# Seven block products on two halves of a 512-token group instead of on pairs of groups, w_out resident in SBUF, and the weight conversion's products on VectorE

## The chip, the cores and the metric

The kernel runs on one core of a Trainium2 chip. The metric is the device time of one execution in microseconds (us); lower is better. The engines are named as in the profile: PE (TensorE matmul), PEld (its weight loads), DVE (VectorE), ACT (ScalarE), POOL (GpSimd), SP (SyncE, which only issues DMAs here).

## The reference

Three layers follow each other: linear attention with an RMS norm, a top-1 mixture of experts, and a wide layer with a cosine gate. The change is in the third, and in the preparation of its weights.

```python
kv = einsum('bhsd,bhse->bhde', k, v); out = einsum('bhsd,bhde->bhse', q, kv)
x = rms_norm(out) * g_norm                    # 4608 tokens x 512
expert_idx = argmax(x @ w_gate, axis=1)       # 8 experts, one for each token
ye = relu(xe @ w1[e]) @ w2[e]; x = gate_w * ye
h = x @ w_in                                  # 512 -> 2048
y = (h * cos(h)) @ w_out                      # 2048 -> 512
```

`w_in` and `w_out` arrive as 64-bit floats (8 MB each), all else in float32.

## The kernel before

Each float32 operand of a large product is split into a high and a low part that TensorE multiplies at full rate; high x high, high x low and low x high (`PASS`) are accumulated. So every product of one 128x128 weight tile is three matmuls.

**Expert stage (205 to 648 us of the trace).** The experts run in an order of falling load, each with a first product (`emit_f1`, L289, eight chunks of two halves) and a second one (`emit_f2`, L302). ACT takes relu of a result (L291) and DVE its low part (L292). Between them the program lays other work by hand: DVE splits w2 (L220), ACT and POOL split the next expert's w1 (L207, L208), POOL gathers the next tokens (L256), and `prep()` advances a generator that converts `w_in` and `w_out` from their 64-bit form, one small chunk at a call. In a chunk DVE takes exponent and mantissa apart (L850 to L866), ACT makes floats of them (L871, L873), POOL multiplies (L874, L875: 64 products of 128x512) and, for `w_in`, forms sums of blocks on POOL (L897: 16 of 128x512; L905 to L908: 32 of 128x256). The results go to DRAM (`win`, `wout`).

**Last stage (648 us to the end).** `x @ w_in` is computed by Strassen's method in Winograd's form: two blocks of K (256 each), two blocks of the 2048 columns, and two blocks of tokens give seven products instead of eight. In the first 512-token group (`p == 0`) the token blocks are its two halves, so a matmul has 256 columns. The other eight groups are taken in four pairs (`quads`): the token blocks are whole groups, and a matmul has 512 columns. A step `(p, q)` is 84 matmuls of 256 columns or 42 of 512, read from a ring `wi` of five tiles that POOL's DMA queue fills (L998, L1002). The seven results are added into four blocks C11, C12, C21, C22 (DVE, L1294 to L1333; one goes through ACT L1317 and POOL L1318). For each block DVE and ACT compute the cosine (`emit_cos`: DVE L1197, L1198, L1200, ACT Abs and Sin L1202, L1203), DVE multiplies it in (L1206), ACT and DVE split the result (L1221, L1226), and PE multiplies it by `w_out` (`emit_g2`, L1245, twelve matmuls of 512 columns for a block, accumulated in four PSUM banks of a group). A pair has 32 such blocks, sixteen of its first group and then sixteen of its second; blocks of the second group wait in 20 slots. `w_out` is read again for each group through a ring of four tiles (L1011, 144 loads of 512 KB).

The token operands of a pair are loaded (`y_load`), summed on POOL (L972, L979) and split by ACT and POOL (L983, L984) during the pair before: sums in two of its middle steps, one split in its last step but one, and the other six in its last step. One set of operands is shared in a ring of eight places, so that a place is free only when the products of the pair before have read it.

Of the kernel before, what the change touches and what calls it, by code (L numbers as in the profile page):

```python
# [32 lines left out]
def fused_kernel(  # L33
# [13 lines left out]
    nc = tc.nc  # L47
# [787 lines left out]
    def prep_unit(i):  # L835
# [38 lines left out]
        nc.gpsimd.tensor_tensor(out=d[:, 0], in0=mf, in1=ef, op=ALU.mult)  # L874
        nc.gpsimd.tensor_tensor(out=d[:, 1], in0=ml, in1=ef, op=ALU.mult)  # L875
# [13 lines left out]
    def prep_units():  # L889
        G = nc.gpsimd  # L890
        for c in range(C2 // 2):
# [4 lines left out]
            for d, w in ((da, wa), (db, wb)):  # L896
                G.tensor_tensor(out=w.rearrange("p a n -> p (a n)"), in0=d[:, 0].bitcast(F32),  # L897
                                in1=d[:, 1].bitcast(F32), op=ALU.add)
# [6 lines left out]
            G.tensor_tensor(out=wb[:, 1], in0=wb[:, 0], in1=wb[:, 1], op=ALU.add)  # L905
            G.tensor_tensor(out=wb[:, 0], in0=wa[:, 0], in1=wb[:, 0], op=ALU.subtract)
            G.tensor_tensor(out=wa[:, 0], in0=wb[:, 1], in1=wa[:, 0], op=ALU.subtract)
            G.tensor_tensor(out=wa[:, 1], in0=wa[:, 1], in1=wa[:, 0], op=ALU.subtract)  # L908
# [9 lines left out]
    def prep():  # L918
# [471 lines left out]
```

## Time and profile before

| | us |
|---|---|
| median of three runs (lowest, highest) | 1508.56 (1504.46, 1511.31) |
| the profiled execution, its own time | 1508.87 |
| span of its trace, first to last instruction | 1506.5 |
| PE, DVE, POOL, ACT busy in the span | 1356.9, 1145.8, 755.5, 664.9 |
| mean granted TensorE clock | 0.965 of full speed |

The trace has the attention up to about 200 us, the expert stage to 648 us and the last stage to 1498 us, after which only output DMAs run. A busy time counts from an instruction's start to its end, waiting for a port included, so an engine's share is no measure of the work that it has.

### The profile page before, as it was taken

The numbers are of one execution on the slowest core, as the hardware profiler recorded it, in microseconds if no ns is written. First come the engines' busy times: TensorE is split into PE (matmuls) and PEld (weight loads), VectorE is DVE, ScalarE is ACT, GpSimd is POOL, SyncE is SP. The second block draws the span as 40 slices with busy tenths as digits, with TensorE's granted clock in tenths as the row PEclk, the third lists the DMA queues.
The fourth block names the chain that finished last, engine by engine and source line by source line (L and its number), as shares of the span: only waits on it lengthen the run. The fifth ranks groups of instructions, "written<-read, shape, count | busy, mean of one in ns | idle before, by whom it ended". The sixth has DMA issues, their size and how long they took to land.

```text
span 1506.5 us, 22532 instructions
## 1 busy us (share of the span) xinstructions
PE 1356.9 (90%) x7959; PEld 1188.3 (79%) x7959; DVE 1145.8 (76%) x1848; ACT 664.9 (44%) x1308; POOL 755.5 (50%) x869
## 2 busy tenths in 40 slices
PE   7986898999989889967899877999889997999997
PEld 6885788988989889967688656887678876888876
DVE  2898677888787876329979997879887798878751
ACT  4985234454434444414434354433444434434431
POOL 1346347878866656345733446325732347423232
PEclk9998999999999999989999998999989998999999
DMA  9984435676666666575767555767576664666654
GB/s 320 344 278 152 139 121 175 211 229 193 214 215 215 218 207 207 156 227 168 254 207 223 149 146 174 224 184 219 143 242 195 189 206 143 206 186 209 175 179 142
DMA packets 186058, 300.78 MB, mean 200 GB/s; under 512 B 18773, under 2 KB 125317, under 8 KB 184913
## 3 DMA queue, kind: packets, MB, share of 16 engines
q0 software_dynamic: 59392, 191.64, 42.1%
q1 hardware_dynamic: 116624, 97.58, 20.9%
q10 hardware_dynamic: 9920, 10.03, 1.9%
q8 instruction: 66, 1.08, 0.3%
q14 instruction: 56, 0.45, 0.1%
HBM read 247.22 MB, written 51.98 MB: 199 GB/s over the span
## 4 chain that ended last, share of the span: by engine, by line
PE 34%; DVE 12%; POOL 3%; issue 3%; ACT 2%; DMA 1%; POOLq 0%; another core or an unknown queue 0%; DVEq 0%; ACTq 0%
PE acc L1245 19%; PE pr L1186 15%; DVE ni L1197 3%; DVE g L1200 3%; DVE g L1198 2%; POOL xreg L984 2%; DVE g L1206 1%; DMA wi<-win 1%; DVE ha L1322 1%; DVE gg L1226 1%; POOL y L979 0%; ACT wA L983 0%; ACT g L1203 0%; ACT g L1202 0%; POOL wo L1011 0%
## 5 line engine op out<-in xcount | busy, mean ns | idle before, releaser
L1245 PE MATMUL acc<-wo,gg 128*128 128x512 f32 x1728 | 431.2, 400 | 30.8 <-DVE gg L1226 29.2
L1245 PEld LDWEIGHTS acc<-wo,gg 128*128 128x128 f32 x1728 | 331.8, 193 | 110.4 <-DVE gg L1226 35.6
L1202 ACT ACTIVATE g<-g 128x512 f32<-128x512 f32 x144 | 91.0, 632 | 386.9 <-DVE g L1200 386.6
L289 PE MATMUL hp<-xreg,wA 128*128 128x352 f32 (+7 forms) x1536 | 228.1, 308 | 26.5 <-DVE wB L292 25.0
L289 PEld LDWEIGHTS hp<-xreg,wA 128*128 128x128 f32 x1536 | 219.7, 192 | 32.5 <-DVE wB L292 30.7
L302 PE MATMUL yp<-wB,wA 128*128 128x352 f32 (+7 forms) x1536 | 227.5, 306 | 1.8 <-DVE xreg L273 1.5
L302 PEld LDWEIGHTS yp<-wB,wA 128*128 128x128 f32 x1536 | 217.1, 189 | 3.3 <-DVE xreg L273 2.5
L1186 PE MATMUL pr<-wA,wi 128*128 128x512 f32 (+1 forms) x912 | 194.7, 363 | 25.6 <-DMA wi<-win 9.3
L1186 PE MATMUL pr<-xreg,wi 128*128 128x512 f32 x768 | 197.3, 403 | 14.5 <-DVE ha L1333 7.3
L1186 PEld LDWEIGHTS pr<-wA,wi 128*128 128x128 f32 x912 | 154.5, 196 | 54.9 <-ACT p L1317 9.2
L1011 POOL DMA_DIRECT2D wo<-wout x144 | 79.9, 555 | 231.6 <-PE acc L1245 218.8
L1186 PEld LDWEIGHTS pr<-xreg,wi 128*128 128x128 f32 x768 | 147.0, 192 | 51.9 <-DVE ha L1333 9.2
L1226 DVE TENSOR_TENSOR gg<-g,gg 128x512 fp32r<-128x512 f32 x144 | 126.1, 876 | 39.1 <-ACT gg L1221 38.8
L1002 POOL DMA_DIRECT2D wi<-win x128 | 69.4, 543 | 129.0 <-PE pr L1186 124.5
L1200 DVE SCALAR_TENSOR_TENSOR g<-ni,g 128x512 f32<-128x512 int32 x144 | 120.0, 833 | 4.9
L1221 ACT ACTIVATE gg<-g 128x512 fp32r<-128x512 f32 x144 | 87.3, 620 | 44.7 <-PE acc L1245 44.4
L208 POOL TENSOR_TENSOR wA<-w1s,wA 128x512 fp32r<-128x512 f32 x64 | 86.8, 1366 | 39.2 <-ACT wA L207 38.7
L1203 ACT ACTIVATE g<-g,half_pi 128x512 f32<-128x512 f32 x144 | 104.3, 725 | 4.7
L292 DVE SCALAR_TENSOR_TENSOR wB<-hp,wB 128x352 fp32r<-128x352 f32 (+7 forms) x128 | 57.4, 469 | 63.8 <-ACT wB L291 63.7
L291 ACT ACTIVATE wB<-hp 128x352 fp32r<-128x352 f32 (+7 forms) x128 | 52.0, 421 | 82.7 <-PE hp L289 80.3
L1197 DVE TENSOR_SCALAR ni<-hb 128x512 int32<-128x512 f32 x72 | 53.7, 745 | 20.2 <-POOL hb L1318 20.2
L1318 POOL TENSOR_TENSOR hb<-hb,p 128x512 f32<-128x512 f32 x36 | 49.0, 1361 | 32.0 <-ACT p L1317 30.0
(213 smaller groups left out, 2028.1 us busy)
## 6 DMA issues: line engine op xcount, KB each, us to landing
wo<-wout POOLq DMA_DIRECT2D x144, 512.0 KB
wi<-win POOLq DMA_DIRECT2D x124, 512.0 KB
w1s<-in_moe_w_dram SPq DMA_DIRECT2D x64, 256.0 KB
w2s<-in_moe_w_dram SPq DMA_DIRECT2D x64, 256.0 KB
xs<-xo SPq DMA_DIRECT2D x16, 512.0 KB
raww<-in_moe_w_in_dram SPq DMA_DIRECT2D x16, 512.0 KB
win<-xreg POOLq DMA_DIRECT2D x16, 512.0 KB
raww<-in_moe_w_out_dram SPq DMA_DIRECT2D x16, 512.0 KB
```

What stands on the lines that cost most here:

```text
L208: nc.gpsimd.tensor_tensor(out=d[:, 1], in0=t, in1=d[:, 0], op=ALU.subtract)
L289: nc.tensor.matmul(ps, lhsT=wv[:, a, kk, :], rhs=xT[:, b, kk, sl], start=(i == 0 and kk == 0), stop=(i == 2 and kk == KD - 1))
L302: nc.tensor.matmul(ps, lhsT=wv[:, a, kk % 4, :], rhs=hT[:, kk, b, sl], start=(n == 0), stop=(n == 3 * C1 - 1))
L1011: nc.gpsimd.dma_start(wo[n % WO], wout[wo_seq[n]])
L1186: nc.tensor.matmul(ps, lhsT=w[:, a, kk, :], rhs=y[:, b, kk, :], start=(n == 0), stop=(n == 5))
L1197: nc.vector.tensor_scalar(out=ni, in0=h, scalar1=INV_2PI, scalar2=None, op0=ALU.mult)
L1200: nc.vector.scalar_tensor_tensor(out=r, in0=ni, scalar=-PI2_LO, in1=r, op0=ALU.mult, op1=ALU.add)
L1202: nc.scalar.activation(r, r, AF.Abs)
L1203: nc.scalar.activation(r, r, AF.Sin, scale=-1.0, bias=half_pi)
L1221: nc.scalar.activation(gg[:, 0], t, AF.Copy)
L1226: nc.vector.tensor_tensor(out=gg[:, 1], in0=t, in1=gg[:, 0], op=ALU.subtract)
L1245: nc.tensor.matmul(acc[g][t], lhsT=gg[:, a, col * P:(col + 1) * P], rhs=wv[:, b, :], start=(n == 1), stop=(n == 3 * C2))
```

## The change

1. The pairs are gone: all nine groups are computed as the first one was, on two halves, in four steps of 84 matmuls of 256 columns (`steps`, `emit_prod`, L988 in the changed kernel). The blocks C22, C21, C11, C12 of a step belong to the same group and are multiplied by `w_out` in that order. A step's adds are all on DVE (`products`, L1017 to L1039); the detour of one product through ACT and POOL is gone.
2. The operands of the next group are prepared in the three last steps of a group, two, two and three of them at a step (`y_next`, L948 sums and L964 splits, 128x256 each), and have a ring of fourteen places, so that two groups' operands stand side by side. Those of the first group are summed and split on DVE instead of POOL.
3. The first step of the first group is computed inside the last expert's second product.
4. `w_out` stays in SBUF: sixteen loads (four ahead of the loop, four in each of the next three steps) instead of 144.
5. The products and sums of the weight conversion (L874, L875, L897, L905 to L908) go from POOL to DVE.

```diff
-        nc.gpsimd.tensor_tensor(out=d[:, 0], in0=mf, in1=ef, op=ALU.mult)
-        nc.gpsimd.tensor_tensor(out=d[:, 1], in0=ml, in1=ef, op=ALU.mult)
+        nc.vector.tensor_tensor(out=d[:, 0], in0=mf, in1=ef, op=ALU.mult)
+        nc.vector.tensor_tensor(out=d[:, 1], in0=ml, in1=ef, op=ALU.mult)
...
-            G.tensor_tensor(out=wb[:, 1], in0=wb[:, 0], in1=wb[:, 1], op=ALU.add)
+            V.tensor_tensor(out=wb[:, 1], in0=wb[:, 0], in1=wb[:, 1], op=ALU.add)
...
+    NQ = C2 // 4
+    steps = [(g, q) for g in range(NG) for q in range(NQ)]
+    def y_op(g, i):
+        n = 7 * (g % 2) + i
+        t = (xflat, aflat)[n // 8]
+        return t[:, 1024 * (n % 8):1024 * (n % 8) + 1024].rearrange(
+            "p (t k n) -> p t k n", t=2, k=2)
...
+            nc.gpsimd.dma_start(wi[:, n % WI].rearrange("p a t k f -> p a (t k f)"),
+                                win[2 * q:2 * q + 2, :, i].rearrange("c p t k f -> p c (t k f)"))
...
+            add(out=hb[:, 1], in0=hb[:, 1], in1=half["p2"], op=ALU.add)
+            add(out=ha[:, 1], in0=ha[:, 1], in1=half["p4"], op=ALU.add)
...
+                for i in ((), (0, 1), (2, 3), (4, 5), (6,), (), (), ())[u]:
+                    y_split(0, i, nc.vector)
+                for i in ((), (), (), (), (), (0, 1), (2, 3, 4), (5, 6, 7))[u]:
+                    products(0, 0, i)
...
-    gslots = [reg4.tile([P, 512], F32, name=f"g{i}") for i in range(20)]
-    wo = [reg4.tile([P, 2, 512], F32R, name=f"wo{i}") for i in range(WO)]
+    gslots = [reg4.tile([P, 512], F32, name=f"g{i}") for i in range(6)]
+    gg_ring = [wA1[:, 6], wA1[:, 7], reg4.tile([P, 2, 512], F32R, name="gg")]
+    wo = [reg4.tile([P, 2, 512], F32R, name=f"wo{i}") for i in range(C2)]
...
+        products(g, q, 0)
+        if q > 0:
+            y_next(2 * q - 2)
+        emit_g(prev + ("C21",))
+        emit_cos(prev + ("C12",))
+        emit_g(prev + ("C11",))
         emit_split()
         second()
+        products(g, q, 1)
+        if q == 3:
+            y_next(5)
...
+        products(g, q, 4)
+        if q > 0:
+            y_next(2 * q - 1 if q < 3 else 6)
...
+        if q == 0 and g + 1 < NG:
+            y_load(g + 1, wk2)
+        for _ in range(4):
+            if g == 0 and wo_seq:
+                load_wo()
```

Three places show how the instructions moved. On PE at the end of the expert stage (`yp` is the last expert's second product, `pr` a Strassen product, a step's seven being 84 matmuls):

```order
 L302 MATMUL yp<-wB_2156,wA_2161 128x272 x12
 L302 MATMUL yp<-wB_2156,wA_2162 128x272 x12
+L988 MATMUL pr<-xreg,wi 128x256 x48
 L302 MATMUL yp<-wB_2156,wA_2163 128x272 x12
 L302 MATMUL yp<-wB_2156,wA_2164 128x272 x12
+L988 MATMUL pr<-xreg,wi 128x256 x24
 L302 MATMUL yp<-wB_2156,wA_2163 128x272 x12
 L302 MATMUL yp<-wB_2156,wA_2164 128x272 x12
```

Six of the first step's products stand between blocks of the second product, and the seventh follows the last of them; before, all came behind it. On POOL in the last step of a pair, before (L984 is a split, L979 a sum, L1318 the add of one product, `wi` and `wo` loads of weights):

```order
L1002 DMA wi<-win 128x1024
L984 TENSOR_TENSOR wA_170<-yst,wA_170 128x512 x2
L1002 DMA wi<-win 128x1024
L984 TENSOR_TENSOR xreg<-y_9404,xreg 128x512
L984 TENSOR_TENSOR xreg<-y_9405,xreg 128x512
L1011 DMA wo_9399<-wout 128x1024
L984 TENSOR_TENSOR xreg<-t_10464,xreg 128x512
L984 TENSOR_TENSOR xreg<-t_10465,xreg 128x512
L1002 DMA wi<-win 128x1024
L984 TENSOR_TENSOR xreg<-y_9395,xreg 128x512
L984 TENSOR_TENSOR xreg<-y_9396,xreg 128x512
```

And on POOL in the third and fourth step of a group, in the changed kernel:

```order
L975 DMA wi<-win 128x2x512 x3
L964 TENSOR_TENSOR xreg<-t_12017,xreg 128x256 x2
L975 DMA wi<-win 128x2x512 x4
L948 TENSOR_TENSOR yst<-yst 128x256 x2
L964 TENSOR_TENSOR xreg<-yst,xreg 128x256 x2
L975 DMA wi<-win 128x2x512 x3
L964 TENSOR_TENSOR xreg<-yst,xreg 128x256 x2
L975 DMA wi<-win 128x2x512 x2
L948 TENSOR_TENSOR t_12016<-yst,t_12016 128x256 x2
L964 TENSOR_TENSOR xreg<-t_12016,xreg 128x256 x2
```

The adds are of half the width, are spread over three steps of every group, and stand in twos and fours with loads of `wi` between them. On DVE in a first product of the second expert, as a difference (`cd`, `wa`, `wb` are the conversion's tiles):

```order
+L874 TENSOR_TENSOR cd_2644<-c_3276,c_3237 128x512
+L875 TENSOR_TENSOR cd_2644<-c_3278,c_3237 128x512
 L292 SCALAR_TENSOR_TENSOR wB_2156<-hp,wB_2156 128x336 x2
 L220 TENSOR_TENSOR wA_2162<-w2s,wA_2162 128x512
+L897 TENSOR_TENSOR wa<-cd_2643 128x512
+L897 TENSOR_TENSOR wb<-cd_2644 128x512
 L292 SCALAR_TENSOR_TENSOR wB_2156<-hp,wB_2156 128x336 x2
 L220 TENSOR_TENSOR wA_2163<-w2s,wA_2163 128x512
+L905 TENSOR_TENSOR wb<-wb 128x256
+L906 TENSOR_TENSOR wb<-wa,wb 128x256
+L907 TENSOR_TENSOR wa<-wb,wa 128x256
+L908 TENSOR_TENSOR wa<-wa 128x256
```

The conversion's work now stands in DVE's queue ahead of the low parts (L292) for which the second product waits.

## Rows read from the trace of the kernel before

**Rows 1.** The page's first line.
```profile
span 1506.5 us, 22532 instructions
```

**Rows 2.** Windows: stretch, length, busy us (instructions) by engine, clock, DMA share, GB/s.
```profile
205.00:600.00 395.00, 362.60 (x2545) 353.29 (x2544) 313.68 (x421) 180.51 (x368) 285.70 (x255) 0.99 0.66 206
654.00:754.00 100.00, 75.61 (x450) 67.43 (x450) 84.24 (x92) 37.58 (x64) 62.52 (x66) 0.88 0.78 240
1278.00:1439.00 161.00, 161.00 (x692) 130.75 (x691) 127.17 (x208) 68.38 (x114) 51.25 (x81) 0.99 0.64 187
```

**Rows 3.** Timeline of PE: start, us, line, shape, count, [idle before].
```profile
623.72 24.40 PE L302 MATMUL yp<-wB,wA 128*128 128x272 f32 x192
...
652.39 8.86 PE L1186 MATMUL pr<-wA,wi 128*128 128x256 f32 x60 [4.28 <-ACTq L1068]
...
1456.38 41.79 PE L1245 MATMUL acc<-wo,gg 128*128 128x512 f32 x183 [1.02 <-ACT oo L1256]
```

**Rows 4.** Waits of PE, 650 to 1500: first and last of seven.
```profile
PE acc L1245 <- DVE gg L1226: 29.2, 8, 5.7
...
PE pr L1186 <- DVE ha L1322: 1.4, 1, 1.4
```

**Rows 5.** Chain that ended last, in order of time: start, us, piece.
```profile
1143.01 2.81 PE pr L1186 x12
...
1151.36 2.73 PE acc L1245 x12
```

**Rows 6.** Timeline of PE in the first group.
```profile
704.83 2.98 PE L1186 MATMUL pr<-wA,wi 128*128 128x256 f32 x24
707.64 2.98 PE L1245 MATMUL acc<-wo,gg 128*128 128x512 f32 x12
```

**Rows 7.** Timeline of DVE and POOL at 692 us.
```profile
692.60 5.95 DVE L1197 TENSOR_SCALAR ni<-hb 128x512 int32<-128x512 f32 x1
...
693.30 2.53 POOL L972 TENSOR_TENSOR t<-y,y 128x512 f32<-128x512 f32 x2
...
695.78 2.47 POOL L972 TENSOR_TENSOR y<-t,yst 128x512 f32<-128x512 f32 x2
```

**Rows 8.** Timeline of ACT: the first copy of a pair's last step and of the next.
```profile
1063.00 0.57 ACT L1283 ACTIVATE hb<-pr 128x512 f32<-128x512 f32 x1
...
1097.56 0.58 ACT L1283 ACTIVATE hb<-pr 128x512 f32<-128x512 f32 x1
```

**Rows 9.** Timeline of DVE in a step without POOL adds.
```profile
1050.53 0.68 DVE L1307 TENSOR_TENSOR ha<-ha,pr 128x512 f32<-128x512 f32 x1
1051.12 0.42 DVE L1197 TENSOR_SCALAR ni<-hb 128x512 int32<-128x512 f32 x1
1051.58 0.69 DVE L1198 SCALAR_TENSOR_TENSOR g<-ni,hb 128x512 f32<-128x512 int32 x1
1052.30 0.69 DVE L1200 SCALAR_TENSOR_TENSOR g<-ni,g 128x512 f32<-128x512 int32 x1
```

**Rows 10.** POOL by line and shape: count, busy us, mean ns of one, idle before.
```profile
L998 POOL DMA_DIRECT2D wi<-win x28 | 20.0, 723 | 22.2 <-PE pr L1186 21.5 <-DVE g L1206 0.7
...
L984 POOL TENSOR_TENSOR wA<-yst,wA 128x256 fp32r<-128x256 f32 x8 | 5.7, 732 | 8.8 <-ACT wA L983 8.8
```

**Rows 11.** Chain that ended last, at the start of the last stage.
```profile
656.87 11.62 DMA wi<-win
```

**Rows 12.** Windows at the start of the last stage.
```profile
664.00:668.00 4.00, 0.00 (x0) 0.00 (x0) 0.00 (x0) 0.85 (x2) 0.00 (x0) 0.50 1.15 382
```

**Rows 13.** DVE by line, 205 to 600 us.
```profile
L864 DVE TENSOR_SCALAR c<-raww 128x512 int32<-128x512 int32 x32 | 37.1, 1158 | 0.0
```

**Rows 14.** POOL by line, 205 to 600 us.
```profile
L208 POOL TENSOR_TENSOR wA<-w1s,wA 128x512 fp32r<-128x512 f32 x55 | 75.5, 1382 | 32.8 <-ACT wA L207 32.5
...
L874 POOL TENSOR_TENSOR cd<-c,c 128x512 fp32r<-128x512 f32 x24 | 33.6, 1402 | 43.4 <-ACT c L871 43.4
```

**Rows 15.** Waits of PE, 205 to 650 us.
```profile
PE hp L289 <- DVE wB L292: 24.0, 19, 3.5
```

More of the change, by code (lines that the diff above doesn't have):

```diff
@@ L989, in fused_kernel @@
+    wi_seq = [(g, q, i) for g, q in steps for i in range(7)]
     n_wi = [0]
@@ new lines, in emit_prod @@
+    def emit_prod(g, q, i):
+        bank = ps_h("pr") if i != 3 else pt.tile([P, 512], F32, tag="t", name="pr")
+        y = y_op(g, i)
+        m = (g * NQ + q) * 7 + i
+        for f in range(2):
+            ps = bank[:, f * 256:(f + 1) * 256]
+            w = wi[:, m % WI, f]
+            n = 0
+            for a, b in PASS:
+                for kk in range(2):
+                    nc.tensor.matmul(ps, lhsT=w[:, a, kk, :], rhs=y[:, b, kk, :],
+                                     start=(n == 0), stop=(n == 5))
+                    n += 1
+        load_wi()
+        return bank
@@ new lines, in fused_kernel, with products @@
+    gq, wo_seq = [], []
+    for g, q in steps:
+        for nm in ("C22", "C21", "C11", "C12"):
+            fs = 2 * q + (C2 // 2 if nm[1] == "2" else 0)
+            t0 = 2 if nm[2] == "2" else 0
+            gq.append(dict(key=(g, q, nm), g=g,
+                           cols=[(2 * i + j, t0 + j, fs + i) for i in range(2) for j in range(2)]))
+            if g == 0 and nm in ("C21", "C11"):
+                wo_seq += [fs, fs + 1]
+    add = nc.vector.tensor_tensor
+    half = {}
+    def products(g, q, part):
+        if part == 0:
+            ps = emit_prod(g, q, 0)
+            hb = stg.tile([P, 2, 512], F32, tag="raw", name="hb")
+            nc.scalar.activation(hb[:, 1], ps, AF.Copy)
+            half["b"], half["ps"] = hb, emit_prod(g, q, 1)
+        elif part == 1:
+            ha = half["a"] = stg.tile([P, 2, 512], F32, tag="raw", name="ha")
+            add(out=ha[:, 0], in0=half["b"][:, 1], in1=half["ps"], op=ALU.add)
+            half["p7"], half["p5"] = emit_prod(g, q, 2), emit_prod(g, q, 3)
+        elif part == 2:
+            ha = half["a"]
+            add(out=ha[:, 1], in0=ha[:, 0], in1=half["p7"], op=ALU.add)
+        elif part == 3:
+            ha, hb = half["a"], half["b"]
+            add(out=hb[:, 0], in0=ha[:, 1], in1=half["p5"], op=ALU.add)
+            add(out=ha[:, 0], in0=ha[:, 0], in1=half["p5"], op=ALU.add)
+            tiles[g, q, "C22"] = hb[:, 0]
+        elif part == 4:
+            half["p2"], half["p4"] = emit_prod(g, q, 4), emit_prod(g, q, 5)
+        elif part == 5:
+            ha, hb = half["a"], half["b"]
+            add(out=hb[:, 1], in0=hb[:, 1], in1=half["p2"], op=ALU.add)
+            add(out=ha[:, 1], in0=ha[:, 1], in1=half["p4"], op=ALU.add)
+            tiles[g, q, "C11"] = hb[:, 1]
+            tiles[g, q, "C21"] = ha[:, 1]
+        elif part == 6:
+            half["p3"] = emit_prod(g, q, 6)
+        else:
+            ha = half["a"]
+            add(out=ha[:, 0], in0=ha[:, 0], in1=half["p3"], op=ALU.add)
+            tiles[g, q, "C12"] = ha[:, 0]
@@ L1270, in second @@
             emit_g2(*waiting.pop(0))
[L1272 to L1290 removed]
+    y_load(1, wk2)
@@ L1291, in fused_kernel @@
         emit_split()
         second()
[L1293 to L1300 removed]
+        products(g, q, 1)
+        if q == 3:
+            y_next(5)
         emit_split()
[L1302 removed]
+        products(g, q, 2)
```

255 lines of the change are left out of this document (63 added, 192 removed).

## The prediction

> **What bounds the kernel now.** I read the span first [rows 1], then the windows by stage [rows 2], to see which engine a stage waits for. In the expert stage (205 to 600) PE is busy for 362.6 of 395 us, and DVE, at 313.7, is the only other engine near it. In the last stage the stretches differ: from 1278 to 1439 PE is busy for all of 161 us, while from 654 to 754 it has 75.6 of 100 at a mean clock of 0.88. So PE is the bound where nothing disturbs it, and time is lost in places. The timeline gives the stage's ends [rows 3]: the last second product ends at 623.72 + 24.40 = 648.1, the last product with `w_out` at 1456.38 + 41.79 = 1498.2. That is 850.1 us.
>
> How much of it is work? On the chain twelve products of 512 columns take 2.81 us and twelve with `w_out` 2.73 [rows 5], so 0.234 and 0.2275 each. Products of 256 columns follow each other in (707.64 - 704.83) / 24 = 0.117 [rows 6], at full clock. The program has 336 of 256 columns, 1344 of 512, and 1728 with `w_out`: 39.3 + 314.5 + 393.1 = 747 us. Lost are 103. The waits of PE from 650 on are seven groups, of which the first and the last stand in [rows 4], and add to 70.9; the other 32 or so are matmuls at half the clock behind such waits (in the window from 664 to 668 PE did nothing and the granted clock was 0.50, the lower of its two levels, 1.2 of 2.4 GHz [rows 12]).
>
> Why PE waits is seen on DVE and POOL side by side [rows 7]: L1197, 0.42 us long in a quiet step [rows 9], lasted 5.95 us from 692.60, and ended behind two pairs of POOL adds that ran from 693.30 to 698.25. While POOL adds, DVE's operations on SBUF tiles stand still. A pair's last step shows what that costs. Its first copy is at 1063.00 and the next step's at 1097.56 [rows 8]: 34.56 us, against 42 x 0.234 + 48 x 0.2275 = 20.75 of PE's work. In it POOL has fifteen adds of 128x512 at about 1.26 (two took 2.53 [rows 7]), 18.9 us. DVE's own work in a step, by start distances [rows 9]: a block's cosine 0.46 + 0.72 + 0.6 = 1.78, four of them 7.1; eight multiplications and low parts at 0.6, 4.8; six adds, 3.6: 15.5. And 15.5 + 18.9 = 34.4, almost the step's 34.56. So a step takes PE's 20.75 or the sum of DVE's work and POOL's adds, whichever is more.
>
> **The change part by part.**
>
> *Products on halves.* Now 3024 products of 256 columns, 3024 x 0.117 = 353.8, as much as 39.3 + 314.5 before. Cost nothing, by [rows 6], which is this very form. The Trainium skill, "TensorE: Matmul & The Clock Gate", section "Back-to-back issue gap", speaks against it: its sustained spacing is 81 ns at 128 columns and 131 at 512, so, as an estimate from that page, some 98 at 256, and two halves would cost 1.5 times a whole: 176 us more here, 1618 in all. The rows show 117 against 234, exactly one half.
>
> *Steps.* A step is 84 x 0.117 + 48 x 0.2275 = 20.75 us of PE, all 36 alike. DVE has one add more (the one taken from ACT and POOL): 16.1 a step, and two copies of output at a group's end, 1.2.
>
> *Operand preparation.* Each group but the first costs POOL 22 adds of 128x256 at 0.73 [rows 10]: 8, 6 and 8 of them in its three last steps, 5.9, 4.4 and 5.9 us. By the rule above the four steps need 17.3, 22.0, 20.5 and 22.0 us of DVE and POOL together, 81.8, against 83.0 of PE. So PE stays the bound over a group, with an excess of 1.2 us in two steps that the low parts already waiting in the ring of three can cover. I take 2 us for each of eight groups, 16; bounds 0, and 0.73 us of stall for each us of POOL adds, the rate of the pair's last step ((34.56 - 20.75) / 18.9): 0.73 x 16.2 x 8 = 95. I take the low one because that last step held all the adds together, while here the ring of fourteen places lets three steps share them.
>
> *The start.* The overflow branch still holds PE 4.3 us [rows 3]. Before, the first four steps then lost about 31: the chain stood 11.62 us for one load of `wi` [rows 11] behind eight loads of operands, four of `w_out` and more `wi`, 6.5 MB at some 382 GB/s [rows 12], and POOL's adds followed. Now the loads behind the branch are 1 + 2 + 1 MB, some 10 us, and PE has six products (8.4 us) to run meanwhile; but the first block can be multiplied by `w_out` only after DVE has done four cosines, three multiplications, an add and a low part (7.1 + 1.8 + 1.2 = 10.1) and ACT's copies, which wait for the operands' loads. I take 12 with the slow clock behind it; bounds 4 and 31. The first step's 9.8 us of products inside the second product are neither gain nor loss: PE is full there, and they count in the 747. The splits for them go to DVE, which was busy for little there (its second product has no other DVE work), so they cost nothing; if they were late, the branch would come as much later.
>
> *Resident `w_out`.* 128 loads and their POOL issues go; every load now waits for PE's reads, not PE for it, so this gains nothing by itself. `wi` moves more: 252 loads of 512 KB, 28 x 0.72 = 20 us of POOL's issue a group [rows 10], beside 16.2 of adds, well under 83. Five places now hold five products, not ten: between PE's last read of one and the need of its successor lie at least four products and two blocks, 5.6 + 5.5 = 11.1 us. Only the load in the burst of the start took longer. Cost nothing; if that cover went, about 1 us a step.
>
> *Conversion on DVE.* 80 products and sums of 128x512 at 0.6 and 32 of 128x256 at about 0.36 (an estimate by width from the 0.6) are 60 us more for DVE, in its queue ahead of L292. PE already waits there 24.0 us [rows 15]. Against it, POOL's adds leave: the moved lines have 140 us (L874 is the largest, 33.6 of it in one tile), L208 stays with 75.5 [rows 14]. DVE's conversion lines are stretched: L864, an operation like L1197 with its 0.42, has a mean of 1.158 [rows 13], 24 us in 32 instructions, and the seven lines in this way 85. With 140 of 215 us of POOL's adds gone, about 55 of that go too: 60 - 55 = 5. In the first products no POOL add is left at all. I take +3; bounds -15, and +112 if nothing is relieved or hidden (80 x 1.158 + 32 x 0.6).
>
> *Sum.* 648.1 + 3 + 747 + 4.3 + 12 + 16 + 1 (the end's last chain) = 1431.4; outputs behind it as before, 1506.5 - 1498.2 = 8.3: span 1439.7. The profiled execution took 2.4 more than its span: **1442 us**, 4.4% less. That execution (1508.87) is 0.3 above the median, which I leave out.
>
> **Rivals.**
> A. The stall follows POOL's adding time wherever it stands. For it: L1197 and the two-input operations stand in every step, and PE waits in order. Against it: the sum rule gives 81.8 of 83.0. At its full price, 95 in place of 16, 1521 us, slower by 0.8%; half of it gives 1481. It decides the sign from 83 us of stall on.
> B. DVE becomes the bound of the expert stage: the multiplications wait for ACT (L871, L873) in DVE's own queue, with L292 behind them, and PE waits for L292. For it: DVE has 81 us free in 395, mostly in the second products, and 60 come. Against it: the relief. At 112 in place of 3, 1551 us, slower; from about 70 on the gain is gone.
> C. The change does less harm than I charge: start 4, operands 0, expert stage -10: 1405.
> D. The weight load of 128 columns, not the half's stream, sets the pace of the products: PEld has 130.75 us in 691 loads from 1278 to 1439 [rows 2], 0.19 each; 3024 of them are 572 in place of 354, 1660 us. [Rows 6] exclude it unless the clock or the ring changes it. The page named above is of this kind.
>
> **How the numbers follow.** Forecast (1420 to 1465) 0.68. A 0.13: 0.09 between 1465 and 1500, 0.04 near or over 1510. B 0.10: 0.04 still faster and below 1495, 0.01 same, 0.05 slower. C below 1420, 0.06. D 0.01, and 0.02 for a stall that I don't see. The range of 1420 to 1495 holds 0.68 + 0.09 + 0.04 = 0.81. A measurement here can tell about 0.5%, 7.5 us: faster 0.87, same 0.03, slower 0.10.
>
> **What would show it.** Right: PE busy over 95% of the last stage but for its first 20 us; steps of 20.75 us between the first copies in every group, with no step over 23; no L1197 longer than 3.5 us; the end of the expert stage's f1 and f2 work within 5 us of 648 plus the 9.8 of the first step. Wrong: waits of PE for DVE's low parts in every second or third step (A); PE's wait for L292 well over 24.0 with DVE near 95% in first products (B); waits for `wi` after the first group (the ring of five); products of 256 columns over 0.13 apart (D).

## The result, and the profile after

The changed kernel takes **1400.02 us** (median of four runs, 1397.24 to 1402.92) against 1506.51 of the kernel before beside it (1500.63 to 1511.31): a ratio of 0.9295, 95% interval 0.9253 to 0.9337. It is 7.0% faster. The forecast was 1442 us with a range of 1420 to 1465: the sign was right, and the gain was too small by 42 us. The profiled execution of the changed kernel took 1397.95 us, against the forecast's 1442 the same way.

The page's first lines, to be read beside [rows 1] and the small table ahead of the change:

```profile
span 1396.2 us, 25089 instructions
## 1 busy us (share of the span) xinstructions
PE 1330.3 (95%) x9303; PEld 1238.8 (89%) x9303; DVE 1154.4 (83%) x2018; ACT 656.8 (47%) x1328; POOL 599.2 (43%) x755
```

POOL's busy time fell from 755.5 us to 599.2, and DVE's rose by 8.6 only, though 112 operations were handed to it. The windows, in the columns of [rows 2]:

```profile
205.00:600.00 395.00, 379.33 (x2727) 374.01 (x2726) 325.55 (x554) 190.63 (x391) 150.77 (x148) 1.00 0.70 221
654.00:754.00 100.00, 100.00 (x621) 89.93 (x621) 89.42 (x127) 46.15 (x83) 57.15 (x81) 0.98 0.92 267
1162.00:1323.00 161.00, 161.00 (x1018) 145.37 (x1017) 145.49 (x213) 73.00 (x129) 75.83 (x104) 1.00 0.73 193
```

In the expert stage PE is busy for 379.3 of 395 us where it had 362.6. In the last stage it has no gap from 654 us on, where the kernel before had 75.6 of 100. The timeline of PE (start, us, line, shape, count, idle before) has the two ends and the place between them where PE still stood:

```profile
628.45 3.20 PE L302 MATMUL yp<-wB,wA 128*128 128x272 f32 x24
631.49 1.59 PE L988 MATMUL pr<-xreg,wi 128*128 128x256 f32 x12
636.08 7.41 PE L988 MATMUL pr<-xreg,wi 128*128 128x256 f32 x48 [3.01 <-PEq L1079]
645.44 1.69 PE L988 MATMUL pr<-xreg,wi 128*128 128x256 f32 x12 [1.95 <-ACT hb L1013]
651.44 2.90 PE L988 MATMUL pr<-xreg,wi 128*128 128x256 f32 x12 [4.30 <-DVE ni L1188]
...
1386.94 2.88 PE L1236 MATMUL acc<-wo,gg 128*128 128x512 f32 x12
```

The last second product ends at 631.7. Less the 72 products of the first step that now stand inside it (72 x 0.117 = 8.4) that is 623.3, against 648.1 [rows 3]. PE ends at 1389.8. Each of these idle times came once, before the first product of its row. Behind them the chain of work that ended last is PE alone (start, us, piece):

```profile
694.89 2.82 PE pr L988 x24
697.71 2.77 PE acc L1236 x12
700.48 1.41 PE pr L988 x12
```

So 24 products of 256 columns take 2.82 us, 0.1175 each, and twelve with `w_out` 2.73 to 2.77 where 2.73 was counted [rows 5]. Four steps take 83.6 us of PE, 20.90 each (a step's first product starts at 704.46, four steps later one starts at 788.05, with no idle time between), where 20.75 were counted. PE's one large wait in the expert stage (us, times, longest) went from 24.0 [rows 15] to

```profile
PE hp L289 <- DVE wB L292: 14.2, 12, 3.0
```

**Where the 44 us between forecast and profile lie.** Expert stage and what is ahead of it: 648.1 + 3 forecast, 623.3 found, 27.8 less. From there to PE's end: 747 + 4.3 + 12 + 16 + 1 = 780.3 forecast, 766.5 found, 13.8 less. Output tail 6.4 for 8.3, and 1.75 for 2.4 outside the span, 2.6 less. Two terms are to be explained: the conversion (+3) and the operands (16).

### The profile page after: what moved, and what is told of

It reads as the page before. It is cut to its first block, busy times and chain, and to the rows that moved or that the text cites. A ratio compares the mean times of both kernels' runs of the same rounds, so it can differ in the third digit from the quotient of the medians.

```text
span 1396.2 us, 25089 instructions
## 1 busy us (share of the span) xinstructions
PE 1330.3 (95%) x9303; PEld 1238.8 (89%) x9303; DVE 1154.4 (83%) x2018; ACT 656.8 (47%) x1328; POOL 599.2 (43%) x755
## 3 DMA queue, kind: packets, MB, share of 16 engines
q1 hardware_dynamic: 116624, 97.58, 22.7%
## 4 chain that ended last, share of the span: by engine, by line
PE 53%; DVE 1%; issue 0%; ACT 0%; POOL 0%; POOLq 0%; DVEq 0%; ACTq 0%
PE acc L1236 28%; PE pr L988 24%; POOL out_dram L1247 0%; DVE g L1189 0%; DVE ni L1188 0%; ACT g L1193 0%; POOLq L1349 0%; DVE g L1191 0%; ACT g L1194 0%; DVE g L1197 0%; DVE oo L1246 0%; DVE hb L1024 0%; DVE ha L1021 0%; ACT xreg L963 0%; DVE ha L1025 0%
## 5 line engine op out<-in xcount | busy, mean ns | idle before, releaser
L975 POOL DMA_DIRECT2D wi<-win x252 | 181.0, 721 | 370.0 <-PE pr L988 367.1
L1236 PE MATMUL acc<-wo,wA 128*128 128x512 f32 x1152 | 281.7, 394 | 0.0
L988 PEld LDWEIGHTS pr<-xreg,wi 128*128 128x128 f32 x1872 | 235.5, 190 | 16.9 <-DVE ni L1188 4.5
L1236 PEld LDWEIGHTS acc<-wo,wA 128*128 128x128 f32 x1152 | 210.9, 189 | 41.8 <-DVE wA L1217 0.2
L988 PE MATMUL pr<-xreg,wi 128*128 128x256 f32 x1872 | 238.4, 282 | 9.3 <-DVE ni L1188 4.3
L289 PE MATMUL hp<-xreg,wA 128*128 128x352 f32 (+7 forms) x1536 | 225.7, 307 | 15.2 <-DVE wB L292 14.6
L289 PEld LDWEIGHTS hp<-xreg,wA 128*128 128x128 f32 x1536 | 218.6, 191 | 19.8 <-DVE wB L292 18.8
L1193 ACT ACTIVATE g<-g 128x512 f32<-128x512 f32 x144 | 91.1, 632 | 290.9 <-DVE g L1191 290.9
L988 PEld LDWEIGHTS pr<-wA,wi 128*128 128x128 f32 x1152 | 143.1, 188 | 3.8
L988 PE MATMUL pr<-wA,wi 128*128 128x256 f32 x1152 | 145.7, 280 | 0.0
L1236 PE MATMUL acc<-wo,gg 128*128 128x512 f32 x576 | 140.1, 392 | 0.0
L1191 DVE SCALAR_TENSOR_TENSOR g<-ni,g 128x512 f32<-128x512 int32 x144 | 131.2, 911 | 4.9
L1236 PEld LDWEIGHTS acc<-wo,gg 128*128 128x128 f32 x576 | 104.9, 188 | 20.6
L1194 ACT ACTIVATE g<-g,half_pi 128x512 f32<-128x512 f32 x144 | 104.4, 725 | 4.7
L292 DVE SCALAR_TENSOR_TENSOR wB<-hp,wB 128x352 fp32r<-128x352 f32 (+7 forms) x128 | 57.8, 470 | 49.6 <-ACT wB L291 49.5
L1217 DVE TENSOR_TENSOR wA<-g,wA 128x512 fp32r<-128x512 f32 x96 | 70.5, 734 | 3.9 <-ACT wA L1212 3.9
L462 POOL TENSOR_TENSOR xo<-raw,inv 128x512 f32<-128x512 f32 (+1 forms) x40 | 40.9, 1055 | 46.4 <-ACT qT L370 22.9
```

Source lines behind the costliest of these rows:

```text
L289: nc.tensor.matmul(ps, lhsT=wv[:, a, kk, :], rhs=xT[:, b, kk, sl], start=(i == 0 and kk == 0), stop=(i == 2 and kk == KD - 1))
L292: nc.vector.scalar_tensor_tensor(out=hT[:, c, 1, sl], in0=ps, scalar=0.0, in1=hT[:, c, 0, sl], op0=ALU.max, op1=ALU.subtract)
L975: nc.gpsimd.dma_start(wi[:, n % WI].rearrange("p a t k f -> p a (t k f)"), win[2 * q:2 * q + 2, :, i].rearrange("c p t k f -> p c (t k f)"))
L988: nc.tensor.matmul(ps, lhsT=w[:, a, kk, :], rhs=y[:, b, kk, :], start=(n == 0), stop=(n == 5))
L1191: nc.vector.scalar_tensor_tensor(out=r, in0=ni, scalar=-PI2_LO, in1=r, op0=ALU.mult, op1=ALU.add)
L1193: nc.scalar.activation(r, r, AF.Abs)
```

## The experiments

Twelve kernels, each compared with the kernel before on its own chip. The columns: median us, ratio and 95% interval, end of the last second product (less 8.4 us where the first step stands in it), and PE's wait for L292, both from the profiled execution.

| | us | ratio | stage's end | L292 |
|---|---|---|---|---|
| changed kernel | 1400.0 | 0.9295 (0.9253, 0.9337) | 623.3 | 14.2 |
| conv_pool | 1419.4 | 0.9434 (0.9409, 0.9459) | 642.4 | 22.3 |
| conv_only | 1489.0 | 0.9887 (0.9861, 0.9914) | 626.7 | 14.9 |
| conv_both | 1449.3 | 0.9614 (0.9582, 0.9646) | 676.0 | 41.4 |
| w1_dve | 1407.3 | 0.9344 (0.9308, 0.9379) | 634.5 | 16.7 |
| prep_in_f2 | 1418.7 | 0.9422 (0.9393, 0.9450) | 643.6 | 21.4 |
| prep_in_f1 | 1410.2 | 0.9373 (0.9350, 0.9395) | 637.8 | 22.2 |
| ops_one_step | 1456.4 | 0.9662 (0.9632, 0.9692) | 628.8 | 15.2 |
| ops_double | 1439.4 | 0.9546 (0.9512, 0.9580) | 628.8 | 16.0 |
| p2_pool | 1403.8 | 0.9322 (0.9290, 0.9354) | 627.1 | 14.8 |
| wout_reload | 1409.8 | 0.9372 (0.9342, 0.9401) | 622.0 | 13.4 |
| first_step_after | 1401.5 | 0.9306 (0.9279, 0.9333) | 625.1 | 13.5 |
| before_p2_dve | 1489.3 | 0.9900 (0.9858, 0.9941) | 645.3 | 22.9 |

### The conversion: conv_pool, conv_only, conv_both

**conv_pool** undoes part 5 of the change alone.

```diff
-        nc.vector.tensor_tensor(out=d[:, 0], in0=mf, in1=ef, op=ALU.mult)
-        nc.vector.tensor_tensor(out=d[:, 1], in0=ml, in1=ef, op=ALU.mult)
+        nc.gpsimd.tensor_tensor(out=d[:, 0], in0=mf, in1=ef, op=ALU.mult)
+        nc.gpsimd.tensor_tensor(out=d[:, 1], in0=ml, in1=ef, op=ALU.mult)
...
-        G, V = nc.gpsimd, nc.vector
+        G, V = nc.gpsimd, nc.gpsimd
```

> The changed kernel with the products and sums of the weight conversion back on POOL, all else as changed. Theory 1 (the expert stage's 25 us come from POOL's adds leaving the stage): the second product of the last expert ends some 25 us later, PE waits for L292 again about 24 us and not 14, L864 is again over 1.1 us a piece; about 1423 us (1418 to 1428). Theory 2 (the 25 us come from elsewhere: the early start of the stage, other tiles for the overflow branch, variation between executions, and the move is worth the forecast's -3): 1397 to 1403 us.

**conv_only** makes the same edit in the kernel before, the other way round.

```diff
-        nc.gpsimd.tensor_tensor(out=d[:, 0], in0=mf, in1=ef, op=ALU.mult)
+        nc.vector.tensor_tensor(out=d[:, 0], in0=mf, in1=ef, op=ALU.mult)
...
-            G.tensor_tensor(out=wa[:, 1], in0=wa[:, 1], in1=wa[:, 0], op=ALU.subtract)
+            V.tensor_tensor(out=wa[:, 1], in0=wa[:, 1], in1=wa[:, 0], op=ALU.subtract)
```

> The kernel before with the products and sums of the weight conversion on DVE, nothing else changed. Theory 1: 1481 us (1476 to 1488), all of it before the last stage's start. Theory 2: 1500 to 1512 us. My forecast's price for this part was +3 us: 1509.

The move is worth 19.4 us on the changed kernel and, by the ratio 0.9887, about 17 on the kernel before. Theory 1 holds, with some 19 us in place of 25 (conv_only came out a microsecond over its range); theory 2 and the forecast's +3 fall. The rest of the 25 us was between the two executions that were compared: the six kernels with the changed kernel's expert stage end it at 622.0 to 628.8, 625.9 on the mean, and the three with the stage of before (before, before_p2_dve, conv_pool) at 642.4 to 648.1, 645.3 on the mean: 19.4 apart.

Is it POOL's adding itself, or work that stood behind it? **conv_both** leaves the conversion on DVE and adds on POOL as often as before, on a tile that nothing else reads.

```diff
         nc.vector.tensor_tensor(out=d[:, 1], in0=ml, in1=ef, op=ALU.mult)
+        pool_add()
+        pool_add()
...
+    def pool_add(n=512):
+        nc.gpsimd.tensor_tensor(out=scr[:, 0, 0:n], in0=scr[:, 1, 0:n], in1=scr[:, 1, 0:n],
+                                op=ALU.add)
```

> The changed kernel with the conversion's products and sums on DVE as changed, and as many adds of the same shapes on POOL at the same places of the program, on a scratch tile that nothing else reads. Theory 1a (POOL's adds themselves, running beside DVE's operations on SBUF, held DVE and so PE): the 19 us of conv_pool come back and DVE's new work adds to them, 1419 to 1450 us, L864 again near 1.1 us. Theory 1b (not the adds, but that their results came late in POOL's queue behind ACT's copies, and work stood behind them): 1398 to 1405 us, since nothing waits for these adds.

It is the adding: 49 us slower than the changed kernel, though nothing reads a result of these adds. POOL's queue, with its other work behind the adds, does not account for it: in this stage neither PE nor DVE waits for POOL, and ACT does for 10.6 us, against 5.2 in the changed kernel. DVE by line from 224 to 598 us (count, busy us, mean ns, idle before; L220 the low parts of w2, L881 and L905 the products and sums of the conversion, L292 the low parts that PE waits for):

```profile
L292 DVE SCALAR_TENSOR_TENSOR wB<-hp,wB 128x336 fp32r<-128x336 f32 (+5 forms) x94 | 41.0, 465 | 10.6 <-ACT wB L291 9.0 <-issue 1.4
L220 DVE TENSOR_TENSOR wA<-w2s,wA 128x512 fp32r<-128x512 f32 x47 | 37.8, 804 | 0.5
...
L881 DVE TENSOR_TENSOR cd<-c,c 128x512 fp32r<-128x512 f32 x22 | 22.6, 1028 | 1.2 <-ACT c L879 0.8
...
L905 DVE TENSOR_TENSOR wb<-cd 128x512 f32<-128x512 f32 x8 | 10.6, 1330 | 0.0
```

In the changed kernel the line of L881 (L875 there) has 688 ns and L220 691. L292, which has one operand in PSUM, keeps its length (465 here, 464 there): what PE waits for is not stretched itself, it stands in DVE's queue behind what is. One number of the expectation missed: the line of L864 was not near 1.1 us but at 615 ns (205 to 600 us); here the adds met other operations of DVE.

### DVE's room in the stage: w1_dve, prep_in_f2, prep_in_f1

If POOL's adds do harm, the last of them should go too. **w1_dve** gives the low parts of w1 to DVE.

```diff
-        nc.gpsimd.tensor_tensor(out=d[:, 1], in0=t, in1=d[:, 0], op=ALU.subtract)
+        eng = nc.vector if nsplit[0] > 2 * C1 else nc.gpsimd
+        eng.tensor_tensor(out=d[:, 1], in0=t, in1=d[:, 0], op=ALU.subtract)
```

> The changed kernel with the low parts of w1 (L208, 56 of 128x512 in the expert stage) on DVE too, so that POOL adds nothing from the second expert on. Theory 1a: POOL's 75 us of adds leave, the stretched L864 and L220 come down to 0.45 and 0.6, 34 us of new DVE work come: 1388 to 1398 us, PE's wait for L292 below the 14.2 of the changed kernel. Theory 2 (DVE is at its limit in the first products, 307 of 374 us busy): PE waits for L292 longer, 1405 to 1420 us.

Neither theory as it stood. The stretching went, as the first said: the line of L864 came to 421 ns. But the time did not fall; the second theory's numbers came true (1407 us, and 16.7 of wait for L292), though the difference is not clear of the noise (0.9344 against 0.9295, intervals that overlap; the stage's end is later than in any of the six). DVE by line, 224 to 600 us:

```profile
L209 DVE TENSOR_TENSOR wA<-w1s,wA 128x512 fp32r<-128x512 f32 x51 | 35.2, 690 | 49.6 <-ACT wA L207 49.5
```

DVE stood 49.6 us for ACT's copy of w1, with the rest of its queue behind. That wait was POOL's before. So DVE was held by ACT's copy and not, as the second theory had it, by its own work alone.

The other two deal the conversion's chunks out in another way: **prep_in_f2** six to a first product and twelve to a second one, **prep_in_f1** twelve and six; the changed kernel has ten and eight.

```diff
-                for _ in range(2 if c % 4 == 3 else 1):
+                if c % 4 != 1:
                     prep()
...
-            prep()
+            for _ in range(1 + u % 2 if r > 0 else 1):
+                prep()
```

> The changed kernel with the conversion's chunks dealt out six to a first product and twelve to a second one, not ten and eight. Theory 1 (what PE still waits for L292, 14.2 us, is DVE's queue in the first products, and second products have room): the first products of experts 1 to 6 get shorter by 1 to 2 us each, 1390 to 1396 us. Theory 2 (the wait is for something else, POOL's w1 parts or ACT): 1398 to 1405 us.

> The changed kernel with twelve of the conversion's chunks in a first product and six in a second one (none in its last two blocks), the other way round from prep_in_f2. Theory 1 (DVE's backlog at the end of a second product is what PE pays at the first low parts behind it): the first wait for L292 in each first product goes, 1390 to 1398 us. Theory 2 (DVE has no room in the first products either, so twelve chunks there make PE wait in the middle of them): PE's waits for L292 over 20 us, 1405 to 1420 us.

Both are slower. With the chunks in the second products (+19 us) PE waits once in each first product (twice in one of them), until 7 to 10 us after its start and for long; the timeline of PE at two of them:

```profile
295.94 24.20 PE L289 MATMUL hp<-xreg,wA 128*128 128x316 f32 x156 [4.16 <-DVE wB L292]
...
481.28 22.51 PE L289 MATMUL hp<-xreg,wA 128*128 128x288 f32 x156 [4.52 <-DVE wB L292]
```

That is a backlog of DVE carried over from the second product, where PE waits for little of DVE's (6.5 us in all). With the chunks in the first products (+10) PE has eighteen waits in place of twelve, in the middle of them. So the first theory fell in both. In prep_in_f1 the second held (22.2 us of wait, 1410 us); in prep_in_f2 it fell too, since the wait is still for L292. DVE's order is near a balance, and neither product has room.

### The operands: ops_one_step, ops_double, p2_pool, before_p2_dve

**ops_one_step** prepares all seven operands in a group's last step, as the pairs nearly did.

```diff
-        if q > 0:
-            y_next(2 * q - 2)
+        if q == 3:
+            y_next(0, 1)
...
-        if q == 3:
-            y_next(5)
+        if q == 3:
+            y_next(2, 3)
...
-        if q > 0:
-            y_next(2 * q - 1 if q < 3 else 6)
+        if q == 3:
+            y_next(4, 5, 6)
```

> The changed kernel with all seven operands of the next group prepared in the group's last step, as the pairs were, not in its three last steps. Theory 1 (a step takes the larger of PE's 20.75 us and the sum of DVE's work and POOL's adds): the last step has 17.3 us of DVE and 16.2 of POOL, 33.5, so 12.7 us over in each of eight groups, less a little that waiting blocks cover: 1485 to 1505 us, the lost time in PE's waits for DVE's low parts. Theory 2 (the operands cost nothing now because the halves' ring of fourteen places and PE's order took the stall away, however the adds stand): 1397 to 1410 us.

It costs 56 us, less than the rule of the sum (85 to 105), far more than nothing. The last step has 28.2 us between its first copy and the next step's (781.10 and 809.31), where the rule says 33.5. The timelines of ACT, DVE and POOL in it:

```profile
787.05 0.42 ACT L963 ACTIVATE xreg<-t 128x256 fp32r<-128x256 f32 x1 [4.74 <-POOL t L948]
...
789.34 0.61 ACT L1212 ACTIVATE wA<-g 128x512 fp32r<-128x512 f32 x1
```

```profile
789.99 0.69 DVE L1217 TENSOR_TENSOR wA<-g,wA 128x512 fp32r<-128x512 f32 x1 [6.73 <-ACT wA L1212]
...
795.67 1.22 DVE L1217 TENSOR_TENSOR wA<-g,wA 128x512 fp32r<-128x512 f32 x1
...
798.12 5.50 DVE L1188 TENSOR_SCALAR ni<-ha 128x512 int32<-128x512 f32 x1
```

```profile
797.72 1.46 POOL L964 TENSOR_TENSOR xreg<-yst,xreg 128x256 fp32r<-128x256 f32 x2
799.12 1.44 POOL L948 TENSOR_TENSOR t<-yst,t 128x256 f32<-128x256 f32 x2
800.52 1.43 POOL L964 TENSOR_TENSOR xreg<-t,xreg 128x256 fp32r<-128x256 f32 x2
801.91 1.42 POOL L964 TENSOR_TENSOR xreg<-yst,xreg 128x256 fp32r<-128x256 f32 x2
```

PE's waits for the low parts from 650 us on are eight, one at the end of the last step of each of eight groups:

```profile
PE acc L1236 <- DVE wA L1217: 21.4, 5, 4.3
PE acc L1236 <- DVE gg L1217: 13.7, 3, 5.2
```

Two things come together ahead of them. ACT stands 4.74 us for POOL's sum (L948), and behind that copy in ACT's queue is the block's high part (L1212), for which DVE stands 6.73 us. And L1188 meets eight adds in a row and ends at 803.6 behind the last of them (803.3), 5.08 more than its 0.42; the other stretched operations there lose half a microsecond each. So the lost time hangs on order and on what meets what.

**ops_double** keeps the spread and does each of POOL's operand adds twice.

```diff
-            engine.tensor_tensor(out=d[:, 1, kk], in0=t, in1=d[:, 0, kk], op=ALU.subtract)
+            for _ in range(2 if g > 0 else 1):
+                engine.tensor_tensor(out=d[:, 1, kk], in0=t, in1=d[:, 0, kk], op=ALU.subtract)
```

> The changed kernel with each of POOL's operand adds of groups 1 to 8 done twice (the second result is the same or is not used). A group then has 64.4 + 1.2 of DVE's work and 2 x 17.9 of POOL's adds. Theory 1 (a group takes the larger of PE's 83.0 us and the sum of both): 101.4 against 83.0, eight times 18.4: 1530 to 1550 us. Theory 2 (the price of ops_one_step, 56 us for eight times 17.9 in one step, 0.39 us for each us of POOL's adds): 1450 to 1460 us. Theory 3 (POOL's adds cost PE nothing while they are spread): 1398 to 1405 us.

All three miss: 39 us, a quarter of what the sum rule gives and two thirds of the second price. ACT's waits from 720 to 1380 us (us, times, longest) show a way:

```profile
ACT xreg L966 <- POOL t L951: 46.3, 16, 4.8
...
ACT wA L966 <- POOL t L951: 35.0, 12, 4.8
ACT xreg L966 <- POOL yst L951: 13.3, 8, 1.9
...
ACT wA L966 <- POOL yst L951: 10.0, 6, 1.9
```

104.6 us; the same four waits have 43.8 in the changed kernel. ACT is waiting for POOL's sums, and the blocks' copies behind it in its queue come late: DVE's waits for them rise from 6.2 to 23.8 us from 654 us on, and PE has 34 short waits for low parts and copies, 17.4 us in all, where it had none. DVE's operations are stretched more as well (see the next kernel); how the 39 us divide between the two is not shown.

**p2_pool** brings back ACT and POOL for the fifth product.

```diff
+                nc.scalar.activation(p2, half["p2"], AF.Copy)
+                nc.gpsimd.tensor_tensor(out=hb[:, 1], in0=hb[:, 1], in1=p2, op=ALU.add)
...
-            add(out=hb[:, 1], in0=hb[:, 1], in1=half["p2"], op=ALU.add)
```

> The changed kernel with the fifth product of each step added into its block by ACT and POOL again (a copy by ACT, an add of 128x512 on POOL), and three places instead of four for output rows, for room. DVE has 0.6 us less a step, POOL 1.26 more. Theory 1 (the sum over a group): 63.2 + 1.2 + 17.6 + 5.0 = 87 against 83.0, up to 4 us a group, so 1415 to 1435 us. Theory 2 (the adds cost only what they stall of DVE's stretchable operations, and there is room left): 1398 to 1405 us.

1403.8, no difference that can be measured: theory 2. It also shows that stretching alone need not cost anything. What DVE's operations from 720 to 1380 us last beyond the shortest of their line (over 0.1 us each) comes to 119 us here. It is 85 in the kernel before, 70 in the changed one, 95 in ops_double, and 45 in ops_one_step, which has the least of it and loses the most of the three variants. In the kernel before the same detour did cost. There DVE waited three times for that one add, in pairs' last steps; its waits from 650 to 1500 us, and the timeline at the second of them:

```profile
DVE ni L1197 <- POOL hb L1318: 20.2, 3, 7.8
```

```profile
1082.55 1.76 DVE L1206 TENSOR_TENSOR g<-hb,g 128x512 f32<-128x512 f32 x1
1090.47 3.79 DVE L1197 TENSOR_SCALAR ni<-hb 128x512 int32<-128x512 f32 x1 [6.17 <-POOL hb L1318]
```

PE too waited three times for the detour, for ACT's copy (L1317), which stood in ACT's queue behind copies that waited for POOL's sum (L979). PE's wait, and the timelines of ACT and PE in the same step:

```profile
PE pr L1186 <- ACT p L1317: 15.6, 3, 7.2
```

```profile
1085.57 0.63 ACT L983 ACTIVATE xreg<-y 128x512 fp32r<-128x512 f32 x1 [4.56 <-POOL y L979]
...
1087.32 0.58 ACT L1317 ACTIVATE p<-pr 128x512 f32<-128x512 f32 x1
```

```profile
1087.95 2.93 PE L1186 MATMUL pr<-wA,wi 128*128 128x512 f32 x6 [4.76 <-ACT p L1317]
...
1096.37 4.20 PE L1245 MATMUL acc<-wo,gg 128*128 128x512 f32 x9 [4.64 <-DVE gg L1226]
```

**before_p2_dve** takes it away in the kernel before.

```diff
-        p2 = wk2.tile([P, 512], F32, tag="p2", name="p2", bufs=1)
-        nc.scalar.activation(p2, ps, AF.Copy)
-        nc.gpsimd.tensor_tensor(out=hb[:, 1], in0=hb[:, 1], in1=p2, op=ALU.add)
+        add(out=hb[:, 1], in0=hb[:, 1], in1=ps, op=ALU.add)
```

> The kernel before with the fifth product of each step added into its block by DVE straight from PSUM, not by ACT and POOL. The forecast's rule (a step takes PE's work or the sum of DVE's work and POOL's adds): a pair's last step goes from 15.5 + 18.9 to 16.1 + 17.6, 0.7 us less in three of them: 1503 to 1510 us. Theory of the queue (in the pair's last step DVE stands 6 to 8 us for that one add, which is queued behind POOL's operand adds, three times 20.2 us in all): 1483 to 1493 us.

15 us faster by the ratio, 18 by the medians, as the theory of the queue says. But the three last steps only went from 33.4, 34.6 and 33.3 us to 30.4, 32.7 and 31.4, 7 us together; the rest came in the first group and in other steps of the pairs (22.7 to 19.8, 23.0 to 20.0), which the theory had not named. Nor had it named PE's wait for L1317, which went with the same edit; the two are not separated here.

### The other parts: wout_reload, first_step_after

**wout_reload** loads `w_out` again for every group.

```diff
+        n = steps.index((g, q)) - 2
+        if n >= 0 and steps[n][0] + 1 < NG:
+            for c in (0, 1, C2 // 2, C2 // 2 + 1):
+                load_wo(2 * steps[n][1] + c)
```

> The changed kernel with w_out loaded again for each group into its resident places (128 more loads of 512 KB by POOL's queue, each placed two steps after its tile's last use). Theory 1 (residency gains nothing by itself, the traffic is covered): 1397 to 1404 us. Theory 2 (the traffic left out is what let the loads of wi come in time): PE waits for wi, at least 1 us a step in groups 1 to 8, 1430 us or more.

10 us slower, between the two. PE's waits behind the expert stage:

```profile
PE pr L988 <- DMA wi<-win: 9.7, 3, 3.8
PE pr L988 <- ACT hb L1013: 3.6, 1, 3.6
```

The three waits for `wi` stand before 651.0, 698.2 and 723.2 us. The first is ahead of any added load; before the other two (3.8 and 2.3 us) POOL's queue issues eight loads of `w_out` each time among those of `wi` (from 680 and from 706 us), four first ones and four added. From 724 us to the end there is no wait, with 120 of the 128 added loads still to come. From the stage's end to PE's end the profiled execution has 774.3 us against 766.5 in the changed kernel. So here residency is worth nothing in the steady steps, and 8 to 10 us at the start, where the added loads fall on the first ones.

**first_step_after** puts the first step back behind the overflow branch.

```diff
-                for i in ((), (), (), (), (), (0, 1), (2, 3, 4), (5, 6, 7))[u]:
-                    products(0, 0, i)
...
+    for i in range(4):
+        products(0, 0, i)
+    emit_cos((0, 0, "C22"))
```

> The changed kernel with the first step's products and adds behind the overflow branch again (its operands are still split inside the second product), the cosines between them as in the other steps. Theory 1 (the start's 20 us are DVE's chain of cosines behind the branch, for which PE had only six products as cover): PE now has the first step's seven and the second's six, 18 us of products, to run beside that chain, and loses 8 to 12 us less: 1388 to 1394 us. Theory 2 (the burst of loads sets the start): PE waits for wi instead, 1398 to 1408 us.

No difference (0.9306), and theory 1 fell, theory 2 too: PE now waits for `wi` 0.8 us only. From the stage's end at 625.1 to PE's end at 1391.7 there are 766.6 us, against 766.5 in the changed kernel; so the place of the first step makes no difference. DVE is busy for 6.56 of the 7 us from 641 and for 9.85 of the 10 from 664: DVE is nearly full there, and more products as cover for PE don't change that.

## Why the prediction was right in its sign and wrong in its size

**Conversion, +3: this step failed.** It said "60 - 55 = 5", new work on DVE less relief, as if each microsecond of DVE were one of PE. The three kernels give the two parts apart: DVE's new work with POOL's adds left in place costs 30 us (conv_pool to conv_both, 1419.4 to 1449.3), and POOL's adds leaving give back 49 (conv_both to the changed kernel). So the relief was sized about right, 49 for 55, and the new work was charged twice its price. (The adds in conv_both don't wait for ACT's copies as those of conv_pool do, so the parts are near, not exact.) Much of the rest went into time in which DVE stood: DVE stands 104 of 421 us in conv_pool's stage and 55 of 450 in conv_both's. [Rows 2] have 81 us of that in 395, which the prediction weighed for rival B and left out of its own term. It is -19 where +3 stood, and beyond the bound of -15. Rival B had the sign of this term wrong.

**Operands, 16: this step failed too, on its rule.** "A step takes PE's 20.75 or the sum of DVE's work and POOL's adds" rested on one step, 15.5 + 18.9 = 34.4 against 34.56 [rows 7 to 9]. The match came of a miscount. The split that the program lays at the end of the step before runs on POOL in this one (1062.66): between the two copies POOL begins sixteen adds, 21.7 us, not fifteen of 18.9, and the sum is 37.2, more than the step took. DVE's timeline of that step has eight stretched operations (from 1.67 to 3.79 us, less 0.69 or, for L1197, 0.42 each: 13.6) and 6.17 of waiting for the one add L1318 in POOL's queue. What PE lost there were two waits: 4.76 us for L1317 in ACT's queue and 4.64 for a low part behind L1197 (shown under p2_pool), and behind them its matmuls ran at the lower clock (0.50 granted from 1088 to 1091). ops_double shows the rule false (39 us where it gives 147), ops_one_step too. What costs is a long train of adds that an operation of DVE runs into, and a queue (ACT's, POOL's) in which something that DVE or PE needs stands behind an operand. Spread over three steps both are still there but short: no operation of DVE lasted over 2.51 us from 654 us on (L1188 1.86), ACT waited 43.8 us for sums, and DVE had time for it (the 70 us of stretching above). PE waited for nothing, and the term is 0. The forecast's choice of the lower bound was right, for the reason that it gave (the adds are spread), and the 2 us a group on top of it were not there. Rival A, which is the same rule at full price, fell.

**Start, 12 + 4.3, and PE's work, 747.** From the stage's end to PE's end 766.5 us went by, 19.5 over the 747. Of these 5.4 are the pace: 36 steps at 20.90 in place of 20.75. So the start lost about 14, the branch's 3.0 in them, near the 16.3 that were forecast; 9.3 are PE's three waits; the rest goes with a lower granted clock (0.72 from 636 to 642, 0.82 from 654 to 664). The reason given (DVE's chain of cosines) holds in part: in first_step_after PE has more products as cover and the start is no shorter, with DVE nearly full.

**What was right.** Products on halves at 0.1175 us cost next to nothing (the pace above), and rival D fell; the first step inside the second product is neither gain nor loss (first_step_after); the conversion's relief; PE over 95% busy from 654 us on; no wait for `wi` in the steady steps with a ring of five. Resident `w_out` gains nothing in the steady steps, as said, but 8 to 10 us at the start, which was not said (wout_reload). The sign "no step over 23 us" was badly chosen: the first copies of a group's second and third step are 23.2 apart without any wait of PE, whose own steps are 20.90. The copy of the third comes 2.4 us after its product, behind other work in ACT's queue (L1193, L1194, L1212), where that of the second came at once. Timelines of PE and ACT:

```profile
746.25 1.57 PE L988 MATMUL pr<-xreg,wi 128*128 128x256 f32 x12
```

```profile
750.19 0.58 ACT L1013 ACTIVATE hb<-pr 128x512 f32<-128x512 f32 x1
```

The sign for the end of the expert stage (within 5 us of 648 plus 9.8) failed by 26 us, as the conversion's term did.

Rival C had the direction (start 4, operands 0, expert stage -10, 1405), with 6 in 100.

None of the twelve is faster than the changed kernel.

## What to carry to other kernels

A sum that matches one step is not a mechanism: before it goes into a forecast, count the terms in the timeline of that step, and look there for what each engine stood for. Work moved to an engine that waits for much of its time can cost less than its length (here about 30 us for 60), and adds taken off POOL can give back much (here 49) without standing on any chain, because what they stretch stands ahead of what PE waits for; so don't charge the two one for one. Where DVE has time to spare its stretching can cost nothing (119 us of it in p2_pool). Spread POOL's adds thinly, and keep copies that wait for them out of a queue that carries the blocks.

## What the runs showed of the hardware

How an operation of DVE fares beside POOL's adds depends first on its operands. With one operand in PSUM it kept its length: L1024 0.68 us from 693.74, while POOL added, and none of the seven such lines of the changed kernel (L1017 to L1039) over 0.69 from 654 us on. With operands in SBUF alone it was mostly longer, by very different amounts. Timelines of DVE and of POOL in the changed kernel:

```profile
692.75 1.06 DVE L1197 TENSOR_TENSOR g<-ha,g 128x512 f32<-128x512 f32 x1
693.74 0.68 DVE L1024 TENSOR_TENSOR hb<-ha,pr 128x512 f32<-128x512 f32 x1
...
694.93 1.86 DVE L1188 TENSOR_SCALAR ni<-hb 128x512 int32<-128x512 f32 x1
...
700.08 1.00 DVE L1188 TENSOR_SCALAR ni<-ha 128x512 int32<-128x512 f32 x1
...
763.02 2.50 DVE L1191 SCALAR_TENSOR_TENSOR g<-ni,g 128x512 f32<-128x512 int32 x1
```

```profile
693.15 1.95 POOL L948 TENSOR_TENSOR t<-yst,t 128x256 f32<-128x256 f32 x2
695.07 1.43 POOL L964 TENSOR_TENSOR wA<-t,wA 128x256 fp32r<-128x256 f32 x2
...
700.06 1.61 POOL L964 TENSOR_TENSOR wA<-yst,wA 128x256 fp32r<-128x256 f32 x2 [1.34 <-ACT wA L963]
...
763.54 1.42 POOL L964 TENSOR_TENSOR xreg<-yst,xreg 128x256 fp32r<-128x256 f32 x2
```

L1188, 0.42 us when it is alone, stood through the whole train at 694.93 (it ended at 696.79, the last add at 696.50) and through eight adds in ops_one_step. At 700.08 it got in between two: it ended at 701.08, the first add at 700.79, and the second add took 0.92 us where others take 0.73. L1191, 0.69 alone, stood through two adds at 763.02 to the end of the train. The Trainium skill, "SBUF — State Buffer", section "Who interferes with whom", says that the port pair which VectorE and GpSimd share is an exclusive lock, and of VectorE's two-port modes that whoever issues first has the pair for a whole instruction while the other stands. The rows in which the two take turns agree (1.00 for 0.42 at 700.08, one add); 1.86, 2.50 and 5.50 us, through two adds and more, do not fit one instruction, and there the measurement decides. What lets DVE in between two adds in one case and not in another, no run here shows. The prediction's sentence that DVE's operations on SBUF tiles stand still while POOL adds is so too strong: some stand, some take turns.
